# Cosine of a gated layer with a quarter turn added at the rounding, in a delta-rule attention kernel

## The chip, the core and the metric

The kernel runs on one core of a Trainium2 chip. The metric is the device time of one execution in microseconds. The core has five engines that run side by side and wait for each other by semaphores: TensorE (PE, matrix products; PEld is its loading of weights), VectorE (DVE), ScalarE (ACT), GpSimd (POOL) and SyncE (SP, which issues most DMAs). A profile of one execution gives the start and the duration of every instruction.

## What is computed

A delta-rule attention with a state of 48x48 per head, 4 batches of 8 heads over 768 positions, and behind it a gated layer with 2048 hidden features on the 3072 tokens of 384 features.

```python
for t in range(S):
    kt, vt, bt = (k_n[:, :, t], v[:, :, t], beta[:, :, t, None])
    y[:, :, t] = np.einsum('bhd,bhde->bhe', q[:, :, t], state)
    v_old = np.einsum('bhde,bhd->bhe', state, kt)
    state = state + bt[:, :, :, None] * np.einsum('bhd,bhe->bhde', kt, vt - v_old)
...
h = x @ w_in
g = h * np.cos(h)
return (g @ w_out).astype(np.float32)
```

All inputs and the output are float32, but the two weights of the layer come as float64 and are narrowed on the chip. The change lies in `np.cos(h)`.

## The kernel before

**Attention.** The 768 positions are cut into 24 units of 32 positions. Each unit transposes its keys and queries, forms their products (`gram`), inverts a triangular matrix for two units at a time (`invert`, lines L669 and L676, on GpSimd, for the first pair on VectorE), passes through the state (`through_state` L711, `solve` L742, `update` L765, `within` L782) and gives 128 tokens of features for the layer (`features_out` L809, a ScalarE copy). The units follow each other, since each needs the state of the one before.

**Weights.** While the first units run, the layer's weights are fetched as pairs of 32-bit words in 28 pieces (`narrow_load` L462, on SyncE's queue) and narrowed: ScalarE splits them (L470, L472), VectorE shifts and combines (L476, L481), GpSimd adds (L485). Their buffers have the tag "g", which the gated products share, eight in all.

**Layer.** Two units make a pair p of 256 tokens; there are 12 pairs. The first two pairs compute the hidden features with plain products (`hidden`, L822), the others with a scheme of seven products instead of eight for two of the three blocks of 128 features (`layer` L938, with sums in `layer_out` L954 on ScalarE and L957 on VectorE). The hidden features come in blocks of 128x512, eight for a pair, so 96 in all, each in one of three PSUM banks with the tag "h". They are multiplied by a factor SCALE = 256 against the true h. The output products follow (`output` L964 for the first pair, `product` L1021 for the others, where VectorE forms sums of gated blocks at L1037), and VectorE collects them (`collect`, L1071; the first product by ScalarE, L1058) before the stores (L1082).

**The gate of a block**, four steps, alternating between two engines:

1. `hidden_turns` (L862, ScalarE): h is turned into turns, h / (2 pi), and written as a 32-bit integer, so that it is rounded.
2. `hidden_rest` (L867, VectorE): h / (2 pi) once more, minus the rounded number: a rest between -1/2 and 1/2 of a turn.
3. `hidden_cos` (L874 and L875, ScalarE): the absolute value of the rest, then the sine of pi/2 - 2 pi |rest|, both in place. Its argument lies between -pi/2 and pi/2.
4. `hidden_gate` (L878, VectorE): the cosine times h, into the gated block that TensorE multiplies by w_out.

There are two buffers with the tag "turns" for these steps; the PSUM bank of the block is free after step 4.

**Order.** Each step of all this is a task with an engine, a written cost and a due time (`add`). `Order.run` (L124) plays the program through with these costs and emits each engine's instructions in the order that comes out, then every instruction is pinned behind the one before it on its engine (L1446). Steps 1 to 4 are the tasks "turns", "rest", "cos" and "gate", added by `gating` (L1233) with the written costs 0.65, 0.73, 1.45 and 0.73. So the order of the instructions depends on written numbers, not on what the emitted instructions take on the chip.

Constants are set at the start: `halfpi` (L411), a tile of 128x1, is filled by VectorE, and `warm` (L414) is a first sine on ScalarE before which the activation table is loaded.

Of the kernel before, what the change touches and what calls it, by code (L numbers as in the profile page):

```python
# [11 lines left out]
FP = mybir.dt.float32  # L12
# [3 lines left out]
AF = mybir.ActivationFunctionType  # L16
# [232 lines left out]
def kernel(  # L249
# [32 lines left out]
    nc = tc.nc  # L282
# [17 lines left out]
    const = ctx.enter_context(tc.tile_pool(name="const", bufs=1))  # L300
# [108 lines left out]
    nc.vector.memset(tiny, 1e-6)  # L409
    halfpi = const.tile([128, 1], FP, name="halfpi")  # L410
    nc.vector.memset(halfpi, math.pi / 2.0)  # L411

    warm = const.tile([128, 1], FP, name="warm")
    nc.scalar.activation(warm, halfpi, AF.Sin)  # L414
# [399 lines left out]
    gates, p_hs, turns, rests, p_os, outs = ({} for _ in range(6))  # L814
# [15 lines left out]
    TURN = 1.0 / (2.0 * math.pi * SCALE)  # L830
# [26 lines left out]
    def hidden_of(p, f):  # L857
        return p_hs[(p, f[0], HOME[f[1:]]) if isinstance(f, tuple) else (p, f)]

    def hidden_turns(p, f):  # L860
        turns[p, f] = ffn_pool.tile([128, 4, 128], I32, name="turns")
        nc.scalar.activation(turns[p, f], hidden_of(p, f), AF.Copy, scale=TURN)  # L862

    def hidden_rest(p, f):
        t = turns.pop((p, f))
# [5 lines left out]

    def hidden_cos(p, f):
        r = rests[p, f]
        nc.scalar.activation(r, r, AF.Abs)  # L874
        nc.scalar.activation(r, r, AF.Sin, bias=halfpi, scale=-2.0 * math.pi)  # L875

    def hidden_gate(p, f):
        nc.vector.tensor_tensor(  # L878
# [354 lines left out]
    def gating(p, f, deps, uses, makes, due):  # L1233
        key = (p, f)
        add(("turns", *key), "ACT", 0.65, lambda: hidden_turns(p, f), deps,
            makes=[("turns", ("turns", *key))])
        add(("rest", *key), "DVE", 0.73, lambda: hidden_rest(p, f), [("turns", *key)])
        add(("cos", *key), "ACT", 1.45, lambda: hidden_cos(p, f), [("rest", *key)])
        add(("gate", *key), "DVE", 0.73, lambda: hidden_gate(p, f), [("cos", *key)],
            makes=makes, uses=uses + [("turns", *key)], due=due)  # L1240
# [240 lines left out]
```

## Time and profile before

| | |
|---|---|
| median of four runs | 674.03 us (673.73, 673.93, 674.13, 676.17) |
| the profiled execution | 674.13 us |
| its span, first to last instruction | 672.4 us |
| mean granted clock of TensorE | 0.992 |
| ScalarE, first rounding pass L862 | at 83.1 us |
| ScalarE, last rounding pass L862 | at 647.3 us |
| ScalarE instructions | 510, among them one table load (L414, 1283 ns) |
| VectorE gate L878 | 96 of 681 ns, 65.4 us |
| VectorE rest L867 | 96 of 684 ns, 65.5 us |
| last matmul ends, by the timeline | 667.3 us |

Times in the profile are microseconds unless marked ns. A group of instructions is shown as line, engine, operation, output<-inputs, shapes, count, then busy time and mean ns of one, then the idle time of its engine just before these instructions and what ended most of it. "issue" is idle time in which an engine waited for nothing that the profile shows. A name such as SPq or PEq is an engine's instruction queue. The first 40 us or so TensorE waits for the first units' data; from about 80 us on it works with few gaps.

### The profile page before, as it was taken

The page shows a single profiled execution, that of the slowest core. Times are in us where ns is not written, and L with a number is a line of the kernel's source. Part 1 is how long each engine was busy: PE and PEld are TensorE (multiplying, and loading weights), DVE is VectorE, ACT ScalarE, POOL GpSimd, SP SyncE. Part 2 cuts the span into 40 slices and gives each one's busy share as a digit, 9 for nine tenths or more (in the row PEclk, how much of TensorE's full clock was granted, in tenths as well). Part 3 has the DMA queues.
Part 4 walks back from the last instruction along what each step waited for, and adds up shares of the span by engine and source line. Part 5 has one row for each costly group of instructions (what it writes and reads, how often), then busy time and mean ns, then how long its engine had stood idle before and what let it go on. Part 6 is the DMA issues. An engine that isn't in the chain of part 4 may idle for free.

```text
span 672.4 us, 27309 instructions
## 1 busy us (share of the span) xinstructions
PE 611.4 (91%) x11864; PEld 573.0 (85%) x11864; DVE 475.2 (71%) x912; ACT 295.7 (44%) x510; POOL 348.0 (52%) x734
## 2 busy tenths in 40 slices
PE   4303799999999999999999999999999999999996
PEld 3202687896899999999999999999999999999996
DVE  4799498977676785886876876776766666656661
ACT  3432367672144552653543453444434434434530
POOL 4459797985858318687285383482381680000000
PEclk9999699999999999999999999999999999999999
DMA  8897666455463453534524524516213203000000
GB/s 176 194 194 169 147 133 166 114 104 97 67 100 60 63 98 59 91 57 70 105 40 59 113 33 66 109 25 92 54 26 51 57 3 58 1 5 24 1 24 24
DMA packets 215516, 52.56 MB, mean 78 GB/s; under 512 B 206948, under 2 KB 210164, under 8 KB 215396
## 3 DMA queue, kind: packets, MB, share of 16 engines
q1 hardware_dynamic: 212964, 49.98, 39.3%
q8 instruction: 93, 1.52, 1.0%
q10 hardware_dynamic: 2176, 0.39, 0.4%
q0 software_dynamic: 256, 0.44, 0.3%
q14 instruction: 27, 0.22, 0.1%
HBM read 39.76 MB, written 11.01 MB: 76 GB/s over the span
## 4 chain that ended last, share of the span: by engine, by line
PE 79%; POOL 7%; DMA 4%; SPq 3%; DVE 2%; issue 2%; ACT 1%; DVEq 0%; POOLq 0%
PE p_h L938 29%; PE p_out L1021 28%; PE p_kq L711 4%; PE p_h L822 4%; PE p_out L964 3%; PE p_u L742 2%; PE p_s L765 2%; PE p_kq L782 2%; POOL knrm L514 2%; PE p_g L593 2%; POOL part L669 2%; POOL z L676 2%; PE p_o L1021 2%; DMA pairs<-in_moe_w_out_dram 1%; SPq L369 1%
## 5 line engine op out<-in xcount | busy, mean ns | idle before, releaser
L669 POOL TENSOR_TENSOR part<-z,gb 128x126 f32<-128x126 f32 (+22 forms) x341 | 135.2, 396 | 109.4 <-DMA gb<-g_dr 44.3
L676 POOL TENSOR_TENSOR z<-z,part 128x126 f32<-128x126 f32 (+22 forms) x341 | 139.1, 408 | 26.7
L938 PE MATMUL p_h<-x_ffn,w_in 128*128 128x128 f32 x1120 | 143.6, 276 | 0.0
L938 PEld LDWEIGHTS p_h<-x_ffn,w_in 128*128 128x128 f32 x1120 | 135.5, 192 | 1.3
L1021 PE MATMUL p_out<-w_out,g_ffn 128*128 128x192 f32 x672 | 123.8, 329 | 0.8 <-issue 0.8
L1021 PEld LDWEIGHTS p_out<-w_out,g_ffn 128*128 128x128 f32 x672 | 107.6, 190 | 1.8 <-issue 0.6
L862 ACT ACTIVATE turns<-p_h 128x512 int32<-128x512 f32 x96 | 56.9, 595 | 97.0 <-DVE p_h L957 74.8
L1021 PE MATMUL p_out<-w_sum,g_ffn 128*128 128x192 f32 x496 | 91.5, 329 | 0.0
L1021 PEld LDWEIGHTS p_out<-w_sum,g_ffn 128*128 128x128 f32 x496 | 79.3, 190 | 0.9
L874 ACT ACTIVATE turns<-turns 128x512 f32<-128x512 f32 x96 | 60.4, 629 | 44.5 <-DVE turns L867 44.4
L878 DVE TENSOR_TENSOR g_ffn<-turns,p_h 128x512 f32<-128x512 f32 x96 | 65.4, 681 | 19.9 <-ACT turns L875 17.4
L867 DVE SCALAR_TENSOR_TENSOR turns<-p_h,turns 128x512 f32<-128x512 f32 x96 | 65.5, 684 | 16.0 <-ACT turns L862 15.7
L1037 DVE TENSOR_TENSOR g_ffn<-g_ffn 128x512 f32<-128x512 f32 x88 | 63.3, 720 | 13.3 <-PE p_out L1021 12.7
L875 ACT ACTIVATE turns<-turns,halfpi 128x512 f32<-128x512 f32 x96 | 69.3, 722 | 3.1
L514 POOL TENSOR_TENSOR knrm<-ksum,halves 128x16 f32<-128x16 f32 (+1 forms) x14 | 37.2, 2660 | 64.3 <-DVE ksum L502 64.3
L957 DVE TENSOR_TENSOR p_h<-g_ffn,p_h 128x512 f32<-128x512 f32 x60 | 41.7, 696 | 38.8 <-PE p_h L938 33.2
L954 ACT COPY g_ffn<-p_h 128x512 f32<-128x512 f32 x60 | 35.0, 584 | 73.8 <-PE p_h L938 70.9
L822 PE MATMUL p_h<-x_ffn,w_in 128*128 128x128 f32 x384 | 48.3, 285 | 0.4 <-POOL w_in L485 0.4
L822 PEld LDWEIGHTS p_h<-x_ffn,w_in 128*128 128x128 f32 x384 | 46.0, 199 | 1.6 <-POOL w_in L485 0.6
L1071 DVE SCALAR_TENSOR_TENSOR o<-p_out,o 128x192 f32<-128x192 f32 x74 | 25.2, 353 | 26.6 <-PE p_out L1021 25.1
L938 PE MATMUL p_h<-x_sum,in_sum 128*128 128x128 f32 x320 | 43.7, 280 | 0.0
L938 PEld LDWEIGHTS p_h<-x_sum,in_sum 128*128 128x128 f32 x320 | 39.5, 191 | 1.1
(95 smaller groups left out, 779.9 us busy)
## 6 DMA issues: line engine op xcount, KB each, us to landing
pairs<-in_moe_w_in_dram SPq DMA_DIRECT2D x12, 512.0 KB
gb<-g_dr SPq DMA_DIRECT2D x24, 256.0 KB
pairs<-in_moe_w_out_dram SPq DMA_DIRECT2D x16, 384.0 KB
vp<-in_v_dram SPq DMA_DIRECT2D x96, 48.0 KB
out_dram<-o SPq DMA_DIRECT2D x23, 192.0 KB
z_dr<-z SPq DMA_DIRECT2D x12, 256.0 KB
zt<-z_dr SPq DMA_DIRECT2D x96, 32.0 KB
kp<-in_k_dram SPq DMA_DIRECT2D x128, 24.0 KB
```

Of the source, the lines that this page charges most:

```text
L514: nc.gpsimd.tensor_tensor(out=scales[m][2][:, part], in0=sums[m, part.start][:, 0:n], in1=halves[:, 0:n], op=ALU.pow,)
L669: eng.tensor_tensor(out=part, in0=z[:, 0:rows, j, None].to_broadcast(shape), in1=a[:, j, None, j + 1 :].to_broadcast(shape), op=ALU.mult,)
L676: eng.tensor_tensor(out=behind, in0=behind, in1=part, op=ALU.subtract)
L822: nc.tensor.matmul(p_h[:, i], w_in[:, t, (4 * k + i) * 128 : (4 * k + i + 1) * 128], xts[p][:, t, unit * 128 : (unit + 1) * 128], start=(t ...
L862: nc.scalar.activation(turns[p, f], hidden_of(p, f), AF.Copy, scale=TURN)
L867: nc.vector.scalar_tensor_tensor(out=r, in0=hidden_of(p, f), scalar=TURN, in1=t, op0=ALU.mult, op1=ALU.subtract,)
L874: nc.scalar.activation(r, r, AF.Abs)
L875: nc.scalar.activation(r, r, AF.Sin, bias=halfpi, scale=-2.0 * math.pi)
L878: nc.vector.tensor_tensor(out=place(p, f), in0=step_of(rests.pop((p, f)), f), in1=step_of(hidden_of(p, f), f), op=ALU.mult,)
L938: nc.tensor.matmul(p_h[:, e], in_sum[:, odd_tile, 4 * s + e] if a == "s" else w_in[:, a, f * 128 : (f + 1) * 128], x_sums[p][:, unit] if b ...
L1021: nc.tensor.matmul(p_o, left(p, part, a)[:, e % 4], right(e, b), start=(e == 0), stop=(e == FT // 2 - 1), skip_group_check=True,)
L1037: nc.vector.tensor_tensor(out=left(p, s, to), in0=left(p, s, one), in1=left(p, s, two), op=op)
```

## The change

A new constant tile holds 0.25. Where the turns are rounded (step 1), a quarter is added before the rounding; the function of this pass is Identity with the tile as bias, instead of Copy. The rest of step 2 is then h / (2 pi) minus the nearest integer to h / (2 pi) + 1/4, so it lies between -3/4 and 1/4. The pass with the absolute value in step 3 is gone, and the sine is taken of 2 pi rest + pi/2, between -pi and pi, which is the cosine of h again. Nothing else differs: the tasks, their written costs and the buffers are the same.

```diff
     halfpi = const.tile([128, 1], FP, name="halfpi")
     nc.vector.memset(halfpi, math.pi / 2.0)
 
+    quarter_turn = const.tile([128, 1], FP, name="quarter_turn")
+    nc.vector.memset(quarter_turn, 0.25)
+
...
     def hidden_turns(p, f):
         turns[p, f] = ffn_pool.tile([128, 4, 128], I32, name="turns")
-        nc.scalar.activation(turns[p, f], hidden_of(p, f), AF.Copy, scale=TURN)
+        nc.scalar.activation(
+            turns[p, f], hidden_of(p, f), AF.Identity, bias=quarter_turn, scale=TURN
+        )
...
     def hidden_cos(p, f):
         r = rests[p, f]
-        nc.scalar.activation(r, r, AF.Abs)
-        nc.scalar.activation(r, r, AF.Sin, bias=halfpi, scale=-2.0 * math.pi)
+
+
+        nc.scalar.activation(r, r, AF.Sin, bias=halfpi, scale=2.0 * math.pi)
```

## The prediction

> **What bounds the kernel now.** I read the shares of busy time first, then the chain that ended last, then the costliest ScalarE groups, and then, because a share over the whole span mixes a starting stage with a steady one, the busy time by stage and TensorE's own waits. The page's first part and the chain, TensorE being PE and ScalarE being ACT:
>
> ```profile
> PE 611.4 (91%) x11864; PEld 573.0 (85%) x11864; DVE 475.2 (71%) x912; ACT 295.7 (44%) x510; POOL 348.0 (52%) x734
> ...
> PE 79%; POOL 7%; DMA 4%; SPq 3%; DVE 2%; issue 2%; ACT 1%; DVEq 0%; POOLq 0%
> ```
>
> ScalarE is busy for 44% of the span and holds 1% of the chain; TensorE holds 79%. The first cosine starts at 83 us. So I cut the span there, at 114 us (just behind TensorE's wait at 111.83), at 400, at 640, and at the last matmul's end. Columns: stretch, its length, busy PE, PEld, DVE, ACT, POOL with instruction counts, granted clock, DMA share, GB/s.
>
> ```profile
> 0.00:83.10 83.10, 30.64 (x752) 26.23 (x753) 58.75 (x153) 28.64 (x51) 53.25 (x86) 0.94 0.81 174
> 83.10:114.00 30.90, 28.85 (x740) 25.72 (x739) 27.37 (x50) 21.94 (x43) 25.22 (x30) 1.00 0.63 156
> 114.00:400.00 286.00, 284.78 (x5753) 263.53 (x5752) 216.03 (x398) 133.03 (x229) 184.40 (x408) 1.00 0.46 80
> 400.00:640.00 240.00, 239.79 (x4447) 230.47 (x4447) 159.88 (x288) 106.07 (x179) 85.16 (x213) 1.00 0.22 40
> 640.00:667.40 27.40, 27.31 (x179) 27.01 (x178) 12.92 (x25) 6.06 (x10) 0.00 (x0) 1.00 0.08 19
> ```
>
> TensorE's idle time, stretch minus busy: 52.5 us before any cosine exists, then 2.05, 1.22, 0.21 and 0.09 us, 3.57 us in all from the first cosine to the last matmul. After that come 5.0 us with one VectorE collect and the last store. These 3.57 us are nearly all that any engine beside TensorE can give back here. Who ended them, from 83.1 us on (total, times, longest):
>
> ```profile
> PE p_t L562 <- issue: 1.4, 1, 1.4
> PE p_out L1021 <- issue: 0.8, 1, 0.8
> PE p_h L822 <- POOL w_in L485: 0.4, 1, 0.4
> PE p_t L562 <- ACT x_ffn L809: 0.2, 1, 0.2
> PE p_u L742 <- DMA zt<-z_dr: 0.2, 1, 0.2
> PE p_g L593 <- issue: 0.2, 1, 0.2
> ```
>
> Of the 3.2 us named, 2.4 us are "issue", in which TensorE waits for no engine. No line names the gate (L878). One names ScalarE, a copy of features, with 0.2 us.
>
> Is "busy" here dense work? A matmul's end is modelled, so a wait could hide in it. The tail answers this: from 651.71 us to the end of the matmuls there is only one ScalarE instruction (0.33 us), and the chain has groups of 16 output matmuls at 2.60 us there. At 196.90, 252.35 and 374.62 us, with cosines running, 16 take 2.60 us as well. So gates cost TensorE nothing visible in its rate.
>
> **The change, part by part.** The rows that it touches:
>
> ```profile
> L862 ACT ACTIVATE turns<-p_h 128x512 int32<-128x512 f32 x96 | 56.9, 595 | 97.0 <-DVE p_h L957 74.8
> L874 ACT ACTIVATE turns<-turns 128x512 f32<-128x512 f32 x96 | 60.4, 629 | 44.5 <-DVE turns L867 44.4
> ...
> L875 ACT ACTIVATE turns<-turns,halfpi 128x512 f32<-128x512 f32 x96 | 69.3, 722 | 3.1
> ```
>
> *Removed:* 96 Abs passes (L874) of 629 ns, 60.4 us of ScalarE. In the timeline the sine starts 0.66 us after its Abs (84.72 and 85.38 us), so a gate's way from the rounded rest (L867) to the sine's end becomes 0.66 us shorter.
>
> *Changed:* 96 rounding passes (L862) become Identity with a bias read from a tile. The trace has no Identity. From below it costs what Copy costs now, 595 ns; from above what the dearest ScalarE pass of this size with a bias tile costs, 722 ns (L875). I take 595 plus the difference of the two passes that differ in their bias tile, 722 - 629 = 93 ns: 688 ns, since the source stays in PSUM as in L862. That adds 96 x 93 = 8.9 us (0 to 12.2). Net on ScalarE: -60.4 + 8.9 = -51.5 us (-60.4 to -48.2), 295.7 to about 244 us. A gate's whole way becomes 0.66 - 0.09 = 0.57 us shorter.
>
> *Kept:* the sine, 722 ns. Its argument now goes from -pi to pi, where it went from -pi/2 to pi/2; the 96 sines took 721 to 725 ns over all their data, so the values set no price. It now carries the wait for the rest itself. No sine with a wait stands in the trace; the Abs that waits 44.5 us in total takes 629 ns all the same. I take 0, with the difference of 93 ns as the upper bound (its bias might be read only after the wait), still less than the 660 ns saved.
>
> *Added:* one memset of 128x1 on VectorE. The same memset for halfpi takes 0.06 us at 3.32 us, and VectorE is then idle for 5.54 us until 8.92 us; without this cover it would cost 0.06 us once. The first rounding pass comes at 83 us, so its wait on this memset is over long before. No DMA, matmul or VectorE pass of a gate is added, removed or moved. The written costs of the scheduling tasks stay as they are, so the order of instructions on every engine and queue stays too, but for the absent Abs.
>
> **What of the 51.5 us reaches the end.** From 114 us on ScalarE is busy 239 us of 526 and waits for others; making it faster lengthens these waits. TensorE's work covers it: 524.6 of 526 us busy. Without that cover, each gate's 0.57 us would count, up to 96 x 0.57 = 55 us. VectorE's 17.4 us of waiting for the sine (L875) shrinks, but VectorE is then early for banks that TensorE has no use for yet. The last gate ends at 651.73 us; the output matmuls of the last pair run on without a gap, to the same end.
>
> What is left is the stage from 83 to 114 us, where weights are unpacked over ScalarE, VectorE and GpSimd. Two waits of TensorE there have a cosine upstream:
>
> ```profile
> 85.38 0.72 ACT L875 ACTIVATE turns<-turns,halfpi 128x512 f32<-128x512 f32 x1
> ...
> 84.60 1.40 DVE L550 TENSOR_TENSOR vp<-vp,knrm 128x768 f32<-128x768 f32 x1
> 86.20 0.69 DVE L878 TENSOR_TENSOR g_ffn<-turns,p_h 128x512 f32<-128x512 f32 x1 [0.20 <-ACT turns L875]
> ...
> 92.92 2.50 PE L822 MATMUL p_h<-x_ffn,w_in 128*128 128x128 f32 x20 [0.44 <-POOL w_in L485]
> ```
>
> First, the 0.44 us at 92.92. Going back: the GpSimd add of w_in at 91.26, one of w_out at 90.28, VectorE's shift at 88.75, its combine at 87.67, the state update at 86.81, the gate at 86.20, the sine. The sine can end some 0.57 us sooner, but VectorE is held by L550 until 86.00 (its instructions overlap by 0.09 us, as at 87.67), so the gate moves by 0.29 us at most: gain 0 to 0.29. Second, the 0.24 us at 111.17, where transposes wait for the copy L809, which stood behind two rounding passes (each 0.09 us dearer) and, further up, behind the Abs at 107.50 (0.66 us less). The balance is up to 0.66 - 0.18 = 0.48 us sooner, which caps the gain at 0.24; but 1.36 us of "issue" follow at 111.83, and if that fetch ends at a fixed moment, the gain is 0. Bounds of both together 0 to 0.53; I take 0.3.
>
> Sum, against the profiled execution: its span 672.4 plus 1.73 around it is 674.13 us, 0.10 above the median of the four runs, 674.03. Less 0.3 this is 673.8, and from the median 673.7. **I forecast 673.7 us: no change that can be told** (within 0.3%, 2.0 us, which is about what a measurement of this kernel can tell from none).
>
> [...] The weight loads (PEld) are busy 494.0 of the 526 us from 114 to 640, 94%. [...] The waits of the weight loads from 83.1 us on decide for me; those that end with ScalarE:
>
> ```profile
> PEld p_u L742 <- ACT x_ffn L809: 0.6, 1, 0.6
> ...
> PEld p_u L742 <- ACT turns L875: 0.5, 1, 0.5
> PEld p_g L593 <- ACT turns L862: 0.5, 2, 0.2
> ...
> PEld p_t L562 <- ACT x_ffn L809: 0.4, 1, 0.4
> ```
>
> That is 2.0 us even if each were a true stall of TensorE and all of it vanished. It is my bound for the gain: 674.0 - 2.0 = 672.0.
>
> **Rivals.** *The gates do hold TensorE* (faster). For it: the 2.0 us just named, the 0.4 us behind GpSimd. Against: the matmul rate that is the same with and without cosines. To pass 0.3% all of the 2.0 us and a part of the 0.4 must go: 671.6. Chance 6%.
>
> *Fetches collide* (slower). Gates that end sooner free their g buffers sooner, SyncE's loads of w_out into such buffers start sooner, and with them on the DMA engines TensorE's instructions may come late. For it: TensorE's "issue" waits of 1.36 us at 111.83 and 0.75 us at 173.90, in stretches of 42 to 64% DMA share, and 3.0 us at 72.31 in one of 62%. Against: from 400 us on, at 22% DMA, there is next to none, and the order of loads is the same. One more wait of 1.36 gives 673.7 + 1.4 = 675.1, inside 0.3%; from two on it decides: 673.7 + 2.7 = 676.4, or one like that at 72 us, 676.7. Chance 8%.
>
> *The activation table is switched* (much slower). If Identity were not in the set that the sine uses, each gate would need two loads. The one load in the trace (L414) takes 1283 ns: 96 x 2 x 1.283 = 246 us more on ScalarE, 490 of 672. A gate would get 2.6 - 0.57 = 2.0 us longer; with three hidden banks from which a gate starts every 6.1 us (526 us / 86 gates), I take that half of it is felt, 96 x 1.0 us: 770. It decides as soon as more than two such loads show. Against it: Copy, Abs, Square and Sin share one load now. Chance 2%. [...]
>
> *The edit doesn't do what it says*, with a second pass kept: ScalarE at 295.7 + 8.9 = 304.6 us, and the time still 674.0, since TensorE covers it. It doesn't change the forecast.
>
> **How the numbers follow.** No change to be told: 84%, with 673.7 as its middle, its own range 672.2 (nearly all that ScalarE can release) to 675.4 (one fetch wait of 1.36 and the spread of 0.4 that the three nearest runs before show). Faster 6%. Slower 8 + 2 = 10%. With 672.2 to 675.4 some two in ten are left out, so this is the whole range too.
>
> **What would show it.** In the changed kernel: L874's group gone; L862 at about 688 ns and ScalarE at 244 us busy; one table load; VectorE's wait for the sine well below 17.4 us, ScalarE's waits for VectorE and TensorE longer by most of the 51 us; TensorE busy 611 us again and its idle time from 83 us on between 3 and 5 us. I am wrong on the mechanism if TensorE's busy time itself falls (a wait was hidden in modelled ends), and on the price if "issue" waits grow past 5 us or the stretch before 83 us changes its length.

## The result, and the profile after

Over 53 runs the changed kernel has a median of 674.05 us, over 79 runs beside them the kernel before one of 675.4 us; the ratio of their means (673.78 and 675.51) is 0.9974, with a 95% interval of 0.9963 to 0.9986. That is 1.76 us of 675.4 (0.9 to 2.5): within the forecast's 0.3%, but its interval leaves out no change at all. The 79 runs go from 670.89 to 680.81 us, with a standard deviation of 2.0 us (the changed kernel: 1.8); the four runs shown before happened to lie close together. The profiled execution of the changed kernel took 676.37 us, near the upper end of its runs (669.51 to 676.78), so its span of 674.6 us says nothing against the ratio.

The page after, busy shares and chain:

```profile
PE 613.5 (91%) x11864; PEld 573.4 (85%) x11864; DVE 476.0 (71%) x913; ACT 246.2 (36%) x414; POOL 349.1 (52%) x734
...
PE 80%; DMA 5%; DVE 5%; POOL 4%; SPq 3%; issue 2%; ACT 1%; DVEq 0%; ACTq 0%
```

ScalarE fell by 49.5 us, from 44% to 36%, and its 1% of the chain is as it was. Its groups, and VectorE's gate (line, form, count, busy, mean ns of one, idle before, what ended it):

```profile
L865 ACT ACTIVATE turns<-p_h,quarter_turn 128x512 int32<-128x512 f32 x96 | 66.0, 687 | 130.3 <-DVE p_h L963 96.2
...
L881 ACT ACTIVATE turns<-turns,halfpi 128x512 f32<-128x512 f32 x96 | 69.1, 721 | 45.4 <-DVE turns L872 45.0
...
L884 DVE TENSOR_TENSOR g_ffn<-turns,p_h 128x512 f32<-128x512 f32 x96 | 65.0, 679 | 7.8 <-ACT turns L881 6.9
```

The rounding pass has grown from 595 to 687 ns. The sine, which now does the waiting itself, kept its 722 ns. What ScalarE saved has become waiting: its idle time ahead of the rounding pass went from 97.0 to 130.3 us. VectorE's wait for the sine fell from 17.4 to 6.9 us. The stretches, in the columns of the prediction's table (PE, PEld, DVE, ACT, POOL busy, clock, DMA share, GB/s):

```profile
83.10:114.00 30.90, 27.94 (x728) 24.53 (x727) 26.50 (x49) 18.25 (x35) 25.52 (x30) 0.99 0.57 142
114.00:400.00 286.00, 283.21 (x5730) 260.99 (x5729) 214.92 (x393) 106.91 (x179) 184.62 (x405) 1.00 0.45 79
400.00:640.00 240.00, 240.00 (x4451) 230.87 (x4451) 160.94 (x291) 85.90 (x140) 85.89 (x215) 1.00 0.22 41
```

TensorE idles 2.96, 2.79 and 0 us: no less than before. So this profile shows ScalarE's work gone and nothing of it at the end, while the ratio says that 1.8 us went somewhere.

A busy row can hide part of such losses. TensorE at 110 us, in this profile (start, length, line, form, count, idle before):

```profile
110.26 0.66 PE L565 MATMUL p_t<-consts,kp 128*128 128x128 f32 x4 [0.87 <-ACT x_ffn L812]
112.40 0.66 PE L565 MATMUL p_t<-consts,qp 128*128 128x128 f32 x4 [1.48 <-issue]
112.89 4.44 PE L970 MATMUL p_out<-w_out,g_ffn 128*128 128x384 f32 x8
```

Behind two pauses, eight output matmuls take 4.44 us, against 2.75 for the same eight in the second profile of this kernel. The granted clock was 0.5 from 113.2 to 116.6 us. The matmul row calls none of that idle.

### The profile page after: what moved, and what is told of

Its sections match the earlier page's. It is cut to its first block, busy times and chain, and to the rows that moved or that the text cites. A ratio compares the mean times of both kernels' runs of the same rounds, so it can differ in the third digit from the quotient of the medians.

```text
span 674.6 us, 27226 instructions
## 1 busy us (share of the span) xinstructions
PE 613.5 (91%) x11864; PEld 573.4 (85%) x11864; DVE 476.0 (71%) x913; ACT 246.2 (36%) x414; POOL 349.1 (52%) x734
## 3 DMA queue, kind: packets, MB, share of 16 engines
q1 hardware_dynamic: 212964, 49.98, 38.4%
## 4 chain that ended last, share of the span: by engine, by line
PE 80%; DMA 5%; DVE 5%; POOL 4%; SPq 3%; issue 2%; ACT 1%; DVEq 0%; ACTq 0%
PE p_h L944 29%; PE p_out L1027 28%; PE p_kq L714 4%; PE p_h L825 4%; PE p_out L970 3%; PE p_s L768 2%; PE p_u L745 2%; PE p_kq L785 2%; PE p_g L596 2%; PE p_o L1027 2%; SPq L369 1%; DMA pairs<-in_moe_w_out_dram 1%; DVE p_i L679 1%; DVE part_v L672 1%; POOL knrm L517 1%
## 5 line engine op out<-in xcount | busy, mean ns | idle before, releaser
L672 POOL TENSOR_TENSOR part<-z,gb 128x126 f32<-128x126 f32 (+22 forms) x341 | 131.0, 384 | 106.0 <-DMA gb<-g_dr 71.4
L679 POOL TENSOR_TENSOR z<-z,part 128x126 f32<-128x126 f32 (+22 forms) x341 | 144.2, 423 | 26.7
L865 ACT ACTIVATE turns<-p_h,quarter_turn 128x512 int32<-128x512 f32 x96 | 66.0, 687 | 130.3 <-DVE p_h L963 96.2
L884 DVE TENSOR_TENSOR g_ffn<-turns,p_h 128x512 f32<-128x512 f32 x96 | 65.0, 679 | 7.8 <-ACT turns L881 6.9
L714 PEld LDWEIGHTS p_kq<-st,kq_t 48*32 48x32 f32 x2944 | 29.5, 107 | 7.5 <-issue 6.3
```

The lines of the kernel that those rows point to most:

```text
L672: eng.tensor_tensor(out=part, in0=z[:, 0:rows, j, None].to_broadcast(shape), in1=a[:, j, None, j + 1 :].to_broadcast(shape), op=ALU.mult,)
L679: eng.tensor_tensor(out=behind, in0=behind, in1=part, op=ALU.subtract)
L714: nc.tensor.matmul(p_kq[quarter(b), par, a, j], kq_t[rows48(par), a, b * NP + j], st[rows48(par), b // 2, j, b % 2], start=(j == 0 and a = ...
L865: nc.scalar.activation(turns[p, f], hidden_of(p, f), AF.Identity, bias=quarter_turn, scale=TURN)
L884: nc.vector.tensor_tensor(out=place(p, f), in0=step_of(rests.pop((p, f)), f), in1=step_of(hidden_of(p, f), f), op=ALU.mult,)
```

## The experiments

All share the kernel before, on the same chip in each batch. Ratios are to it, with 95% intervals.

**1. More passes in some gates.** If ScalarE's removed pass gave the gain, adding passes should show where. Two kernels add, in each gate, three copies of the rest onto itself to the changed kernel, in the first two pairs or in the others; the result is the same.

```diff
         r = rests[p, f]
+        for _ in range(3 if p in ONES else 0):     # early3; late3: p not in ONES
+            nc.scalar.activation(r, r, AF.Copy, scale=1.0)
         nc.scalar.activation(r, r, AF.Sin, bias=halfpi, scale=2.0 * math.pi)
```

> The changed kernel with three more ScalarE passes per gate (a copy of the rest onto itself, about 630 ns each, result unchanged) in the first two pairs alone: 16 gates, 48 passes, 30 us of ScalarE work between 80 and 160 us. Theory A (what the change gains, 0.26% or 1.7 us, comes from the stage of the first two pairs, where ScalarE stands in the chain of the weights' narrowing): there 16 fewer passes gave 1.7 us, so three more passes lose at least 3 x 1.7 = 5 us against the changed kernel, ratio to the kernel before 1.005 or above. Theory B (the gain comes from waits in the steady stage that the modelled ends of matmuls hide): as the changed kernel, ratio 0.996 to 0.999. Theory C (the gain comes from elsewhere: another place of the tiles in memory, or fewer instructions to fetch): ratio 0.996 to 0.999 too.

> The changed kernel with three more ScalarE passes per gate from the third pair on: 80 gates, 240 passes, 151 us of ScalarE work, ScalarE at about 397 us of the span. Theory A: TensorE covers it, the ratio stays near the 0.997 of the changed kernel, up to 1.000. Theory B: 80 passes less gave 1.7 us, so 240 more lose 5 us or more (a gate gets 1.9 us longer): ratio 1.005 or above. Theory C: 0.996 to 0.999.

Measured: 1.0094 (1.0065 to 1.0123) early, 1.040 (1.0371 to 1.0429) late. Theory A had asked for the first loss alone and theory B for the second alone; both came. TensorE's waits, first in the early kernel from 83 to 180 us, then in the late one from 130 us on (total, times, longest):

```profile
PE p_t L565 <- ACT x_ffn L812: 3.5, 2, 2.4
PE p_out L970 <- ACT o L982: 2.1, 1, 2.1
...
```

```profile
PE p_h L944 <- DVE g_ffn L884: 8.0, 10, 1.6
PE p_z L804 <- ACT y L796: 4.1, 6, 1.7
PE p_out L1027 <- DVE g_ffn L884: 2.7, 2, 1.4
...
```

In the early kernel ScalarE's copies end TensorE's longest waits, in the late one the gate (L884) and such a copy; neither the kernel before nor the changed one lists a wait of TensorE for the gate. So enough extra work breaks through the cover. It doesn't follow that the pass taken away had been on the path, which is what the next two asked.

**2. The two parts of the change apart.** One kernel has the new constant and its memset alone; the other leaves out the pass with the absolute value and changes nothing else.

```diff
     nc.vector.memset(halfpi, math.pi / 2.0)
+    quarter_turn = const.tile([128, 1], FP, name="quarter_turn")    # const_only
+    nc.vector.memset(quarter_turn, 0.25)
...
-        nc.scalar.activation(r, r, AF.Abs)                          # no_abs
```

> The kernel before with the new constant tile and its memset, and nothing else: every later tile moves in memory, no ScalarE pass changes. Theories A and B: ratio 1.000, within 0.1%. Theory C, in its form that the place of the tiles does it: 0.997.

> The kernel before without the pass with the absolute value (the rounding pass stays a Copy, so the cosine is wrong for negative rests; the computation leaves that pass out). ScalarE work 295.7 - 60.4 = 235 us, 9 us less than in the changed kernel. Theories A and B: the removed pass is the whole gain and the bias of the rounding pass costs a seventh of it at most, so ratio 0.996 to 0.998. Theory C by place of tiles: 1.000.

Measured: the constant alone 0.9977 (0.9955 to 0.9999, just clear of 1), the pass left out 1.0016 (0.999 to 1.0042). Theories A and B had wanted the reverse, and fall. A tile that no instruction reads gives the gain; 60 us less of ScalarE gives none. The tile takes 32 bytes of each partition and moves every tile behind it: w_in from byte 47840 to 47872, z from 159968 to 160000, o from 212192 to 212224. All of these ended up as multiples of 64. The tiles ahead of it, kp and qp among them, stay. The engines' own instructions don't get faster by it: with the constant alone the rounding pass, the sine and the gate take 595, 722 and 681 ns, as before.

**3. The change without the shift, and shifts without the change.**

```diff
-    halfpi = const.tile([128, 1], FP, name="halfpi")
+    both = const.tile([128, 2], FP, name="halfpi")                  # after_unmoved
+    halfpi, quarter_turn = both[:, 0:1], both[:, 1:2]
...
+    pad = const.tile([128, 1], FP, name="pad")                      # pad32; pad64: [128, 16]
+    nc.vector.memset(pad, 0.25)
```

> The changed kernel, but with the 0.25 in a second column of the tile that holds pi/2, so that no other tile moves in memory (w_in starts at byte 47840 of a partition as before; in the changed kernel at 47872, a multiple of 64). All the arithmetic of the change, none of the shift. Theory C (the whole gain comes from the 32 bytes by which the tiles move, since DMA transfers to addresses that are multiples of 64 take less time): ratio to the kernel before 1.000 (0.999 to 1.002), share of the DMA queue q1 39.0% or more as in the kernel before and in the one without the Abs. Rival A (ScalarE's saved passes give the gain): 0.997, whatever the DMA share.

> The changed kernel once more, beside the others on the same chip: ratio 0.997 (0.996 to 0.999) by both theories, q1 at 38.0 to 38.7%.

> The kernel before with an unused tile of 128x1 and its memset: tiles from there on move by 32 bytes to multiples of 64, ScalarE does all it did (the same program as the one with the constant alone, under another name). Theory C: ratio 0.9975 again, q1 at 38.0 to 38.7%. Rival A: 1.000.

> The kernel before with an unused tile of 128x16 (64 bytes a partition) and its memset: the tiles move by 64 bytes, so w_in at 47904 is again not a multiple of 64. Theory C, multiples of 64: ratio 1.000, q1 at 39.0% or more. If any shift, or the memset, did it: 0.9975. Rival A: 1.000, whatever the DMA share.

Measured: the change with unmoved tiles 1.0008 (0.9984 to 1.0032); the change as it is 0.9962 (0.9949 to 0.9975); a shift by 32 bytes 0.9987 (0.9966 to 1.0009); a shift by 64 bytes 1.0017 (0.9995 to 1.0039). The share of the DMA queue q1 was 38.7, 38.4, 38.7 and 39.1%: the first missed its expected 39.0%, the others met theirs. The shift by 32 bytes is the same program as the constant alone; its interval holds both the 0.9975 and the 1.000 that were to be told apart. The shift by 64 bytes has the additional tile and memset too, and no gain, so the memset is not it. The share takes in every packet of the queue and the length of the span, so I summed packet times by size instead (table below). The unmoved kernel has all of the new arithmetic:

```profile
L864 ACT ACTIVATE turns<-p_h,halfpi 128x512 int32<-128x512 f32 x96 | 65.9, 688 | 130.4 <-DVE p_h L962 95.1 <-PE p_h L943 25.6 <-PE p_h L824 9.0
```

and TensorE's waits from 130 us on, there and in the moved kernel's second profile:

```profile
PE p_u L744 <- DMA zt<-z_dr: 3.1, 5, 1.3
PE p_out L1026 <- issue: 0.8, 1, 0.8
PE p_g L595 <- issue: 0.5, 1, 0.5
...
```

```profile
PE p_out L1027 <- issue: 1.1, 2, 0.8
PE p_g L596 <- issue: 0.6, 1, 0.6
PE p_u L745 <- DMA zt<-z_dr: 0.3, 1, 0.3
...
```

The unmoved kernel waits 3.1 us for tiles zt that come late from memory, the moved one 0.3. Its timeline shows that such a wait can cost more than itself:

```profile
247.46 0.24 PE L744 MATMUL p_u<-rhs,zt 32*32 32x48 f32 x2 [0.93 <-DMA zt<-z_dr]
248.02 0.27 PE L744 MATMUL p_u<-rhs,zt 32*32 32x48 f32 x2 [0.32 <-DMA zt<-z_dr]
248.59 0.27 PE L744 MATMUL p_u<-rhs,zt 32*32 32x48 f32 x2 [0.31 <-DMA zt<-z_dr]
249.07 0.75 PE L744 MATMUL p_u<-rhs,zt 32*32 32x48 f32 x58 [0.21 <-DMA zt<-z_dr]
249.75 4.55 PE L1026 MATMUL p_out<-w_sum,g_ffn 128*128 128x192 f32 x16
```

1.77 us of waits, and then 16 matmuls take 4.55 us where 2.77 is their length elsewhere: from 250.00 to 253.40 us the granted clock is 0.50. These are single profiles; one kernel's profile with late tiles isn't yet its mean. And 3.1 us is the exception: in the other ten profiles of the table below these waits come to no more than 0.9 us, with 0.2 us in the kernel before, whose tiles lie where the unmoved kernel has them. So the place alone doesn't bring them.

**4. Which tiles, how large a multiple, how much cover.** The first two put the unused tile ahead of the attention's work tiles or of the layer's tiles (with a second one behind the first group, so that only one group moves to the better place); the third shifts all by 96 bytes; the last adds two passes to every gate of the changed kernel.

```diff
+    pad_w = work.tile([128, 1], FP, name="pad_w", bufs=1)           # work_only, with pad_f too
+    nc.vector.memset(pad_w, 0.25)
+    pad_f = ffn_pool.tile([128, 1], FP, name="pad_f", bufs=1)       # ffn_only: this alone
+    nc.vector.memset(pad_f, 0.25)
     bq = ffn_pool.tile([128, NU, C], FP, name="bq", tag="g", bufs=GATES)
...
+    pad = const.tile([128, 24], FP, name="pad")                     # pad96
...
+        for _ in range(2):                                          # two_more
+            nc.scalar.activation(r, r, AF.Copy, scale=1.0)
```

> The kernel before with one unused 32-byte tile ahead of the pool of the attention's work tiles and one ahead of the layer's tiles: only the work tiles (g, gb, z, zt, vp) come to multiples of 64, the weights and the layer's tiles (o, pairs, gates) stay at odd multiples of 32. ScalarE does all it did. Theory C1 (the transfers of the attention's tiles through memory, z and zt above all, are what TensorE waits for): ratio 0.998, and the packets of 128 bytes at 87 us in sum over 16 engines instead of 90, those of 1536 at 17.3 as before. Theory C2 (the stores of o or the weights' pairs matter): 1.000.

> The kernel before with the unused tile ahead of the layer's tiles alone: only they come to multiples of 64. Theory C1: ratio 1.000, packets of 128 bytes at 90 us, those of 1536 (stores of o) at 16.1 instead of 17.3. Theory C2: 0.998.

> The kernel before with an unused tile of 96 bytes: tiles move to multiples of 64 that are not multiples of 128 (z at 160064). Theory C with multiples of 64: ratio 0.998, packets of 128 bytes at 87 us, of 1536 at 16.1. If multiples of 128 are wanted: 1.000 and 90 us, 17.3 us.

> The changed kernel with two more ScalarE passes for every gate (a copy of the rest onto itself, 630 ns each, result unchanged), one more pass than the kernel before has: ScalarE at about 367 us. If one pass less gave nothing because TensorE's work covers it, the cover should hold a part of one pass more: ratio 1.000 to 1.010, against 1.0094 for three more in the first two pairs and 1.040 for three more in the others. If the time went linearly with passes (4% for 240 passes), 192 more would give 1.030 over the changed kernel, 1.027.

Measured: work tiles alone 0.9994 (0.9971 to 1.0017), the layer's tiles alone 0.9976 (0.9953 to 0.9999), 96 bytes 0.9985 (0.9955 to 1.0014), two more passes 1.0006 (0.9985 to 1.0027). The runs without additional passes in one table: where z and o start, modulo 256; the summed time in us of the DMA packets of 128 and of 1536 bytes, divided by the 16 DMA engines, in one profile each; and the time in that profile from the 1801st matmul (at 128 to 132 us) to the last.

```
kernel           Abs    z    o   128 B  1536 B   steady   ratio
before           yes  224  224   90.20   17.28   538.1    1
no_abs           no   224  224   89.72   17.33   541.8    1.0016
after_unmoved    no   224  224   90.21   17.49   543.4    1.0008
pad64            yes   32   32   88.79   17.67   540.8    1.0017
pad96            yes   64   64   89.16   17.37   540.3    0.9985
work_only        yes    0   32   87.35   17.53   539.1    0.9994
ffn_only         yes  224    0   90.17   15.94   538.3    0.9976
const_only       yes    0    0   87.37   16.15   538.1    0.9977
pad32            yes    0    0   87.26   16.01   536.8    0.9987
the change       no     0    0   87.29   16.12   539.6    0.9974
after_again      no     0    0   86.97   15.93   539.7    0.9962
```

The packet times follow the places. The 128-byte packets take 87.0 to 87.4 us where z starts at a multiple of 256 and 88.8 to 90.2 elsewhere; the 1536-byte ones (2944, which is 128 for each of the 23 whole stores of o) take 15.9 to 16.2 us with o at such a multiple, and 17.3 to 17.7 elsewhere. The three kernels with more passes, whose tiles lie as in the change, agree: 87.1 to 87.4 and 16.0 to 16.3 us. A multiple of 64 isn't enough: the 96-byte shift has that, and neither packet time falls below the range of the other places (89.16 and 17.37 us). So for the packets theory C holds, but not with the 64 that I had given it (these places can't tell 128 from 256 for a start at 0, and only show that 32, 64 and 224 are worse). Among these worse places the start made little difference for the 1536-byte packets: 17.53 and 17.67 us at 32, 17.28 to 17.49 at 224. Why the packets take longer in sum from these places is not shown.

For the time, the five kernels with o at a multiple of 256 have ratios of 0.9962 to 0.9987, the five others 0.9985 to 1.0017. Weighted by their intervals the means are 0.9972 and 1.0005, with standard errors of 0.0004 and 0.0006, not counting that the ratios of a batch share the runs of the kernel before. Without that kernel: the 42 runs of the four kernels with o at a multiple of 256, the change's own 53 left out, have a mean of 674.1 us, the 60 of the five others 675.6, 1.5 us apart (0.7 to 2.4). In experiment 2 alone it is 2.1 us, in experiment 3 2.0, in experiment 4 0.6 with 1.4 either way, so that experiment settles little by its times. The steady times point the same way (538.5 and 540.6 us on average), with single profiles that overlap. Theory C1, which had put it down to the attention's tiles, found its packet times but not its ratio: 0.9994 with them moved, 0.9976 without. The two intervals overlap, and the two medians, 675.19 and 674.24 us, lie closer than the runs of either spread (1.6 and 1.9 us as a standard deviation), so which tiles matter is not settled.

Nor is it shown how the shift shortens the kernel. One part can be read: from the end of the last matmul to the end of the span, where the last store of o stands, the six kernels with o elsewhere take 5.04 to 5.15 us and the five with o at a multiple of 256 take 4.84 to 4.88. That is 0.2 of the 1.8 us. The rest stands in no place that these profiles tell from their own scatter.

Two more passes on every gate, 1.0006: 0.37% over the two means of the changed kernel (0.9969 together), 2.5 us (some 1.5 either way, by the two intervals) for 192 passes of 629 ns, 121 us, as expected. So the kernel before is far from using up the cover. With three more in the first two pairs it is used up.

## Why the prediction was right, and where its reasons were not

- **The number.** Part of it is luck. 673.7 against a median of 674.05 is closer than the parts: the starting point of 674.03, from four runs, was 1.4 us under the 675.4 of 79 runs, and the gain was 1.76 us instead of 0.3. The two errors cancel.
- **What bounds the kernel.** Right. TensorE covers ScalarE's passes: with the pass gone and nothing moved, 1.0016 and 1.0008; with two more, 2.5 us of 121. Nor did taking ScalarE's passes away shorten the 32 us between 114 and 640 us in which no weight load was busy (526 less 494.0): in the profile after they are 34 (526 less 491.86). The Abs' own share of the gain comes out of two comparisons. With moved tiles 0.9969 without it and 0.9980 with it (three kernels, in one of them only the layer's tiles moved), a difference of -0.11%; with unmoved ones +0.12% (no_abs and after_unmoved against 1). Each has a 95% interval of about 0.17% either way. Together that is 0.0 with some 0.8 us either way, and the 0.3 us that I forecast for it can't be told from nothing.
- **The prices on ScalarE.** Rounding pass 688 ns, measured 687; sine with the wait 722, measured 721; ScalarE busy 244 us, measured 246.2. One table load, VectorE's wait for the sine down, ScalarE's own waits up: as written.
- **The added memset.** This is the step that failed. I priced it as an instruction, 0.06 us under 5.54 us of cover, and wrote that no DMA "is added, removed or moved". The tile it fills moves the tiles behind it by 32 bytes, and the shift, not the arithmetic, goes with the 1.8 us: 0.9977 and 0.9987 with the tile alone, 1.0008 for the arithmetic without the shift. No price in my sum stood for it. The forecast held since the missing term, 1.8 us, was smaller than the range of 2.0; its interval, to 2.5, reaches past that.
- **TensorE's idle time as the bound of any gain.** The 3.57 us were one execution's, and a good one: in the stretch from the 1801st matmul the eleven profiles lie between 536.8 and 543.4 us. Late DMAs (0.2 to 3.1 us of waits for zt) and half-clock stretches (3.4 us at 113 us in one of the changed kernel's two profiles) come and go from one profile to the next, and my 0.4 us for the spread came from three runs; it is 2.0 us as a standard deviation. Two signs that the prediction named came out wrong in the one profile after: TensorE's idle time from 83.1 us to the last matmul was 2.96 + 2.79 = 5.75 us, not 3 to 5, and the stretch before the first rounding pass was 81.66 us long instead of 83.12. The second had been named as a sign of a wrong price; with the 1801st matmul anywhere from 127.8 to 132.4 us in the eleven profiles, neither can be told from the scatter.
- **"Busy is dense."** Half right. The matmul rate doesn't depend on the gates (16 output matmuls in 2.60 us with cosines running and without, in the kernel before), but a stretch at half clock is busy too: 4.55 us for what takes 2.77. A test of the rate at three places in one profile couldn't see that.
- **The rivals.** *Gates hold TensorE*: out, by the kernels without the pass. *Fetches collide*: in the one profile after, TensorE's "issue" waits from 83 us on are 1.5 + 0.8 + 0.3 = 2.6 us against 2.4; not seen. *Table switch*: one load; out. But the fetch rival asked the right question, what else moves, of the wrong thing.

## What to carry to other kernels

When an edit adds a tile, look at where every tile behind it lands, and test the edit once with the tile in a place that moves nothing: here that alone turned 0.997 into 1.001. Adding work to an engine shows when that engine's cover (the other engine's work that hides it) breaks, not whether work taken away was on the path; take the part out by itself. And where a kernel's runs spread by 2 us, one profile's idle time is a sample, not a bound.

## What the runs showed of the hardware

A 32-byte change in where a tile starts, from 224 to 0 modulo 256, changed the summed time of DMA packets by 3% (128 bytes, from 90.08 to 87.25 us on average) and 8% (1536 bytes, from 17.37 to 16.03), in every profile with that place. The median packet of 1536 bytes took 65 ns in all fourteen profiles, so the difference is in the slow ones: the 95th percentile was 281 to 304 ns with o elsewhere and 246 to 267 ns with o at a multiple of 256.

TensorE's granted clock fell to 0.5 for 3.4 us behind pauses of some 2 us: 0.87 and 1.48 us of waits ahead of 113 us in the profile after, 1.77 us ahead of 250 us in the unmoved one. The same place in the changed kernel's second profile, with waits of 0.44 and 1.68 us, kept the full clock, so such pauses can come ahead of it and need not bring it; what decides is not shown. Behind each, the output matmuls took 1.7 to 1.8 us more (4.44 for 2.75, 4.55 for 2.77), on top of the waits. In the clock record of the kernel before, the stretches that end with a change of the clock are 3.413, 10.240 and 590.506 us long, in that of the changed kernel 34.133, 3.413 and 556.372: 1, 3, 173, 10, 1 and 163 times 3.4133 us.

A stretch at half clock stood between 112 and 119 us in seven of the fourteen profiles; it may be one reason for the spread of the runs, but one profile of each kernel can't show that.
